# Seven dk stores as 120 rows meant to leave out DMA engine 4, with seven rows by SyncE and one in pieces, and two as 112 rows: an attention backward kernel on one core

## The chip, the cores and the metric

One core of a Trainium2 chip. The metric is the device time of one execution in microseconds (us). Faster or slower needs 2%. Each experiment was timed in three rounds beside the kernel before, and its 95% interval is given.

## The reference

The reference is the forward pass of attention with one query row per head, and its gradients:

```python
# q: (2, 32, 1, 128); k, v: (2, 32, 8192, 128); grad_out like q; all bfloat16
scores = einsum("bhqd,bhkd->bhqk", q, k) * 128 ** -0.5
p = softmax(scores); out = einsum("bhqk,bhkd->bhqd", p, v)
# returns out, dq, dk, dv
```

There are 64 heads. Each reads 2 MiB of k and 2 MiB of v and writes dk and dv of the same size. That is 8.4 MB a head and 537 MB in all.

## The kernel before

K and V of a head lie in two tiles of 128 partitions by 16 KiB. The kernel keeps twelve such tiles. The gradient overwrites the tile it is computed from and is stored from there. So the load of head i+6 has to wait until the store of head i from the same tile has landed. SyncE issues all loads, in the order of the program. GpSimd issues nearly all stores.

```python
NTILE = 12
FIRST = 6
SPREAD = range(4, 60, 7)
...
    load_eng = nc.sync
    store_eng = nc.gpsimd
...
    def by_rows(eng, dst, src, rows):
        p = 0
        for m in rows:
            pin(eng.dma_start(out=dst[p : p + m], in_=src[p : p + m], max_dma_last_dim=NT * D))
            p += m
...
    for w, a in enumerate((q, grad_out)):
        rows = a.rearrange("b h s d -> (b h s) d")
        r0 = FIRST if w == 0 else 0
        if r0:
            pin(store_eng.inc_swdge_sem([], [], mode="reset_dge_cursor"))
            pin(store_eng.dma_start(out=qd_nat[:r0, w, :], in_=rows[:r0], max_dma_last_dim=D))
        pin(load_eng.dma_start(out=qd_nat[r0:BH, w, :], in_=rows[r0:BH]))
...
    # in outer(), when the last chunk of a gradient tile is done:
            if w == 0 and i in SPREAD:
                by_rows(store_eng, dst, h.tile[w], (P - 2, 2))
            else:
                eng = load_eng if len(ends) > 1 else store_eng
                pin(eng.dma_start(out=dst[:, b0:b1, :], in_=h.tile[w][:, b0:b1, :]))
...
    # in the main loop, per head:
        if (i := at(O1 + NCH)) is not None and i + AHEAD < BH:
            load(i + AHEAD, 0)          # next k, waits for the store of dv of head i
        if (i := at(O0 + NCH)) is not None and i + AHEAD < BH:
            load(i + AHEAD, 1)          # next v, waits for the store of dk of head i
```

A plain store of 128 rows gives each of the sixteen DMA engines eight rows. The special stores of the eight heads in `SPREAD` are there for balance. The 126 rows go to fourteen engines, and the two engines that are left out get one row each. A cursor that GpSimd's transfers carry along decides which two those are. The kernel resets it at the start and moves it by a first load of six small rows.

## Time and profile before

| | before |
|---|---|
| time, median of 4 runs (lowest to highest) | 1281.13 us (1279.28 to 1284.57) |
| span of the profiled run | 1284.2 us |
| share of the DMA engines' time, loads and stores | 49.9% and 48.8% |
| DMA rate of the page | 420 GB/s |
| PE waiting for v loads | 28.8 us in 17 waits |

The lines behind the bound are shown in the prediction below. Three more are needed. The first is GB/s in forty equal slices of the span:

```profile
GB/s 388 427 428 428 428 429 428 427 428 428 428 428 428 420 428 428 428 424 426 428 428 418 425 428 428 422 418 426 428 427 419 422 429 429 426 423 429 428 413 219
```

The second is SyncE's timeline around the first special store (head 4). Its columns are start, length, engine, line and operation, and then the tile written and where it came from.

```profile
120.42 0.33 SPq L100 DMA_DIRECT2D kvt<-in_v_dram  x1
130.48 0.33 SPq L100 DMA_DIRECT2D kvt<-in_k_dram  x1
147.65 0.33 SPq L100 DMA_DIRECT2D kvt<-in_v_dram  x1
157.63 0.33 SPq L100 DMA_DIRECT2D kvt<-in_k_dram  x1
```

The third is from the view of PE's waits (us in total, number, longest).

```profile
PE tp L194 <- DMA kvt<-in_v_dram: 28.8, 17, 5.9
```

### The profile page before, as it was taken

To read this page: it belongs to the slowest core of one execution; us is meant where nothing else is said; L and a number is where in the kernel's file an instruction comes from. 1 tells how busy PE (TensorE), PEld (TensorE's weight loads), DVE (VectorE), ACT (ScalarE), POOL (GpSimd) and SP (SyncE) were. 2 spreads that over 40 slices of the span, in tenths; PEclk is the share of its full clock that TensorE was granted. 3 is DMA by queue.
4 is the path that set the end of the run, shared out by engine and by line. 5 is a ranking of instruction groups with operands and counts; after the bars stand their busy time and mean duration, and the time that the engine had idled before them with its cause. 6 is when DMAs were issued, how large, how long until landed. Compare 5 with 4: busy or idle time off the path is not lost.

```text
span 1284.2 us, 32475 instructions
## 1 busy us (share of the span) xinstructions
PE 1099.4 (86%) x14148; PEld 805.5 (63%) x14148; DVE 1014.6 (79%) x2258; ACT 956.9 (75%) x641; POOL 76.0 (6%) x143
## 2 busy tenths in 40 slices
PE   6899899899889899889899889888888799879870
PEld 5666666666666666666666666666656566656650
DVE  2888888888888888888888888888788688777882
ACT  6777777778778778778778778777778687777750
POOL 0000000000000000000000000000000000000000
PEclk9999999999999999999999999999999899999985
DMA  9999999999999999999999999999999999999995
GB/s 388 427 428 428 428 429 428 427 428 428 428 428 428 420 428 428 428 424 426 428 428 418 425 428 428 422 418 426 428 427 419 422 429 429 426 423 429 428 413 219
DMA packets 40155, 539.03 MB, mean 420 GB/s; under 512 B 5196, under 2 KB 5196, under 8 KB 6476
## 3 DMA queue, kind: packets, MB, share of 16 engines
q1 hardware_dynamic: 20172, 272.70, 49.9%
q0 software_dynamic: 19840, 264.25, 48.8%
q8 instruction: 110, 1.80, 0.5%
q14 instruction: 33, 0.27, 0.1%
HBM read 268.47 MB, written 268.47 MB: 418 GB/s over the span
## 4 chain that ended last, share of the span: by engine, by line
DVE 32%; DMA 17%; issue 14%; another core or an unknown queue 14%; PE 12%; ACT 8%; POOL 1%; SPq 0%; ACTq 0%; POOLq 0%; DVEq 0%
DVE kvt L427 18%; DMA kvt<-in_v_dram 11%; ACT ev L196 8%; PE tp L194 7%; DMA out_dram<-kvt 6%; DVE sel L395 4%; DVE rows L221 3%; DVE sel L389 1%; PE acc L372 1%; DVE pair L303 1%; PE raw L208 1%; ACT E_f L271 1%; DVE dSu L349 1%; PE sw L178 1%
## 5 line engine op out<-in xcount | busy, mean ns | idle before, releaser
L196 ACT COPY ev<-tp 128x2048 bf16<-128x2048 bf16 x512 | 941.3, 1868 | 285.7 <-PE tp L194 280.6
L427 DVE TENSOR_TENSOR kvt<-qb,pair 128x2048 bf16<-128x2048 bf16 x512 | 616.9, 1216 | 0.1
L194 PEld LDWEIGHTS <-kvt 128*128 128x128 bf16 x8192 | 507.0, 102 | 160.7 <-issue 114.4
L194 PE MATMUL tp<-ident_bf,kvt 128*128 128x128 bf16 x8192 | 572.9, 226 | 38.0 <-DMA kvt<-in_v_dram 28.8
L208 PE MATMUL raw<-ev,qdT 128*32 128x512 bf16 x2048 | 210.0, 399 | 5.0 <-ACT ev L196 1.6
L395 DVE SCALAR_TENSOR_TENSOR sel<-acc,diag,sel 128x128 f32<-128x128 f32 x384 | 134.7, 351 | 13.6
L228 PEld LDWEIGHTS sw<-sel,rows 128*128 128x128 f32 x1024 | 124.8, 192 | 29.7 <-issue 12.9
L228 PE MATMUL sw<-sel,rows 128*128 128x16 f32 x1024 | 137.2, 266 | 0.6 <-DVE rl L324 0.6
L372 PE MATMUL acc<-kvt,E_pad 128*32 128x512 bf16 x1024 | 102.9, 391 | 30.6 <-DVE E_pad L280 30.6
L445 POOL DMA_DIRECT2D out_dram<-kvt x118 | 63.3, 536 | 1081.9 <-DVE kvt L427 518.1
L372 PE MATMUL acc<-kvt,dS_pad 128*32 128x512 bf16 x1024 | 111.1, 426 | 0.8 <-DVE dS_pad L358 0.8
L221 DVE COPY rows<-raw 128x512 f32<-128x512 f32 x128 | 87.5, 684 | 26.1 <-PE raw L208 26.1
L178 PE MATMUL sw<-ident_bf,qdT 128*128 128x128 bf16 x128 | 28.5, 223 | 70.9 <-DVE mp L240 70.8
L280 DVE CAST E_pad<-E_f 128x64 bf16<-128x64 f32 x64 | 12.5, 195 | 92.9 <-ACT E_f L271 92.9
L208 PEld LDWEIGHTS <-qdT 128*32 128x32 bf16 x2048 | 64.6, 95 | 25.0 <-issue 18.4
L315 PEld LDWEIGHTS sw<-ld,ones 128*128 128x128 f32 x256 | 38.2, 188 | 54.5 <-issue 29.3
L372 PEld LDWEIGHTS <-E_pad 128*32 128x32 bf16 x1024 | 26.3, 93 | 55.2 <-DVE E_pad L280 40.1
L246 DVE TENSOR_REDUCE gm<-sw 1x1 f32<-1x128 f32 x64 | 17.9, 279 | 49.3 <-PE sw L244 49.3
L409 PE MATMUL acc<-ones,sel 128*128 128x1 f32 x256 | 47.5, 255 | 6.2 <-DVE sel L395 6.2
L315 PE MATMUL sw<-ld,ones 128*128 128x1 f32 x256 | 49.1, 261 | 0.1
L409 PEld LDWEIGHTS acc<-ones,sel 128*128 128x128 f32 x256 | 44.0, 215 | 7.3 <-DVE sel L395 7.3
L389 DVE TENSOR_SCALAR sel<-acc,diag 128x128 f32<-128x128 f32 x128 | 43.8, 342 | 0.0
(49 smaller groups left out, 367.5 us busy)
## 6 DMA issues: line engine op xcount, KB each, us to landing
out_dram<-kvt POOLq DMA_DIRECT2D x118, 2048.0 KB, 51.5
kvt<-in_v_dram SPq DMA_DIRECT2D x64, 2048.0 KB, 19.1
kvt<-in_k_dram SPq DMA_DIRECT2D x63, 2048.0 KB, 19.4
out_dram<-kvt POOLq DMA_DIRECT2D x8, 2016.0 KB, 55.7
out_dram<-kvt SPq DMA_DIRECT2D x8, 512.0 KB, 23.2
kvt<-in_k_dram SPq DMA_DIRECT2D x2, 512.0 KB, 4.5
kvt<-in_k_dram SPq DMA_DIRECT2D x1, 1024.0 KB, 7.2
out_dram<-kvt POOLq DMA_DIRECT2D x8, 32.0 KB, 55.2
```

What stands on the lines that cost most here:

```text
L194: pin(nc.tensor.transpose(tp[:, t, :], src[:, c * CH + t, :], ident_bf[:]))
L196: pin(nc.scalar.copy(out=ev[:], in_=tp[:]))
L208: nc.tensor.matmul(h.raw[g * SW : (g + 1) * SW, :], lhsT=qdT[:, w, q0 : q0 + SW], rhs=ev[:, g * QT : (g + 1) * QT, :].rearrange("p n d -> ...
L221: pin(nc.vector.tensor_copy(out=h.rows[:], in_=h.raw[:]))
L228: nc.tensor.matmul(h.score[w].rearrange("p (n t) -> p n t", t=QT)[:, :, t], lhsT=h.rows[:, t * P : (t + 1) * P], rhs=sel4[:].rearrange("p ...
L315: nc.tensor.matmul(out, lhsT=ones[:].to_broadcast([P, P]), rhs=col, start=True, stop=True)
L372: nc.tensor.matmul(h.acc[w][g : g + CW, :], lhsT=wts[:, n0 : n0 + CW], rhs=rows[:, n0 : n0 + QT, :].rearrange("p n d -> p (n d)"), start=( ...
L389: nc.vector.tensor_scalar(out=h.sel[:], in0=block, scalar1=diag[:, 0:1], scalar2=None, op0=ALU.mult)
L395: nc.vector.scalar_tensor_tensor(out=h.sel[:], in0=block, scalar=diag[:, b : b + 1], in1=h.sel[:], op0=ALU.mult, op1=ALU.add,)
L409: nc.tensor.matmul(h.acc[w][:, 0:1], lhsT=h.sel[:], rhs=ones[:], start=True, stop=True)
L427: nc.vector.tensor_tensor(out=h.tile[w][:, n0 : n0 + CH, :].rearrange("p n (e t) -> p n e t", t=2), in0=h.qb[w][:] .rearrange("p (e t) -> ...
L445: pin(eng.dma_start(out=dst[:, b0:b1, :], in_=h.tile[w][:, b0:b1, :]))
```

## The change

The change wants a finer balance. In seven heads the dk store becomes 120 rows on fifteen engines, which are to leave out engine 4. SyncE stores seven of the eight other rows on the seven lowest engines. The last row is cut: two pieces by GpSimd with 9 and 8 parts of 256 bytes (3 and 2 in head 52) are to bring the cursor back to its place, and SyncE stores the rest. In two late heads 112 rows, 2 rows and twice seven rows are to relieve two more engines.

```diff
-FIRST = 6
-SPREAD = range(4, 60, 7)
+FIRST = 5
+ONE = {4: 9, 12: 9, 20: 9, 28: 9, 36: 9, 44: 9, 52: 3}
+TWO = (57, 61)
...
-            if w == 0 and i in SPREAD:
-                by_rows(store_eng, dst, h.tile[w], (P - 2, 2))
+            if w == 0 and i in ONE:
+                by_rows(store_eng, dst, h.tile[w], (P - 8,))
+                by_rows(load_eng, dst, h.tile[w], (7,), P - 8)
+                a = 2 * ONE[i]
+                for eng, cols in (
+                    (store_eng, slice(0, a - 1, 2)),
+                    (store_eng, slice(1, a - 2, 2)),
+                    (load_eng, slice(a - 1, NT)),
+                ):
+                    pin(eng.dma_start(out=dst[P - 1 :, cols, :], in_=h.tile[w][P - 1 :, cols, :]))
+            elif w == 0 and i in TWO:
+                by_rows(store_eng, dst, h.tile[w], (P - 16, 2))
+                by_rows(load_eng, dst, h.tile[w], (7, 7), P - 14)
```

(`by_rows` gets a fifth argument, the first row. The long call in the loop is joined to one line here.)

More of the change, by code (lines that the diff above doesn't have):

```diff
@@ L83, in slot_of, with by_rows @@
         return n if n < NTILE else slot_of(i - NTILE // 2, 1 - w)
-    def by_rows(eng, dst, src, rows):
-        p = 0
+    def by_rows(eng, dst, src, rows, p=0):
         for m in rows:
@@ L440, in outer @@
             dst = (dv_v if w else dk_v)[i]
-            if w == 0 and i in SPREAD:
-                by_rows(store_eng, dst, h.tile[w], (P - 2, 2))
+            if w == 0 and i in ONE:
[7 more added lines that the diff above has]
+                ):
+                    pin(
+                        eng.dma_start(
+                            out=dst[P - 1 :, cols, :], in_=h.tile[w][P - 1 :, cols, :]
+                        )
+                    )
+            elif w == 0 and i in TWO:
+                by_rows(store_eng, dst, h.tile[w], (P - 16, 2))
+                by_rows(load_eng, dst, h.tile[w], (7, 7), P - 14)
             else:
```

## The prediction

> **What bounds the kernel now.** I read the page from the engines' table to the DMA queues, then the waits of the load queue, the DMA view in two windows, and last the busy time by stretch over the tail.
>
> ```profile
> span 1284.2 us, 32475 instructions
> PE 1099.4 (86%) x14148; PEld 805.5 (63%) x14148; DVE 1014.6 (79%) x2258; ACT 956.9 (75%) x641; POOL 76.0 (6%) x143
> ...
> DMA  9999999999999999999999999999999999999995
> ...
> q1 hardware_dynamic: 20172, 272.70, 49.9%
> q0 software_dynamic: 19840, 264.25, 48.8%
> ```
>
> No compute engine is full, while the two DMA queues (q1 the loads by SyncE, q0 the stores by GpSimd) take 98.7% of sixteen engines' span. One head moves 4 MiB in and 4 MiB out, 8.39 MB; at the 427 GB/s of the window 300 to 400 us that is 19.6 us. Undisturbed compute issues stores every 19.13 us per head (dk stores at 122.85 and 658.40 us, 28 heads apart). So DMA is slower by half a microsecond a head, and the store backlog grows. These are the store lines of the DMA view, first in the window 40 to 140 us, then 900 to 1000 us (count, KB, median us to landing):
>
> ```profile
> out_dram<-kvt POOLq DMA_DIRECT2D x9, 2048.0 KB, 17.2
> ```
>
> ```profile
> out_dram<-kvt POOLq DMA_DIRECT2D x8, 2048.0 KB, 70.5
> ```
>
> The waits of the load queue show the loop closing: a load waits until the store of the buffer that it overwrites has landed, so it waits for the slowest of the sixteen engines.
>
> ```profile
> SPq L100 <- DMA out_dram<-kvt: 1138.7, 116, 25.0
> ```
>
> A landing is sixteen completion marks, one per engine, and the trace keeps their times. For the store issued at 1176.11 us they are: five from 1193.2 to 1199.3, three from 1211.7 to 1215.7, six from 1224.0 to 1228.4, then 1232.4 and 1238.5. The engines are 45 us out of step. At 103 us the spread was only 2.4 us. The tail pays for it (columns: stretch, its length, busy time of PE, PEld, DVE, ACT, POOL, clock, DMA share, GB/s):
>
> ```profile
> 1254.00:1264.00 10.00, 2.77 (x14) 1.39 (x14) 6.82 (x13) 0.00 (x0) 0.00 (x0) 0.50 0.93 389
> 1264.00:1270.00 6.00, 0.00 (x0) 0.00 (x0) 0.00 (x0) 0.00 (x0) 0.00 (x0) 0.50 0.57 235
> 1270.00:1274.00 4.00, 0.00 (x0) 0.00 (x0) 0.00 (x0) 0.00 (x0) 0.00 (x0) 0.50 0.44 177
> 1274.00:1278.00 4.00, 0.00 (x0) 0.00 (x0) 0.00 (x0) 0.00 (x0) 0.00 (x0) 0.50 0.10 40
> 1278.00:1283.00 5.00, 0.00 (x0) 0.00 (x0) 0.00 (x0) 0.00 (x0) 0.00 (x0) 0.50 0.05 21
> ```
>
> Compute is over by 1264 us; for 19 us more a shrinking number of engines drains its backlog, the last 5 us a single one (0.05 is one of sixteen). The work left at 1264 is 6x0.57 + 4x0.44 + 4x0.10 + 5x0.05 = 5.8 us of all engines, so with that work level it would end at 1270, 13 us sooner. That is about what balance can be worth: 1%.
>
> **What the Trainium skill says.** "DMA: Bandwidth & Descriptors", section "Why a DMA increments its semaphore by 16 and not by 1": a transfer runs on the largest k up to 16 that divides its outermost dimension; SyncE's take the lowest-numbered k engines, GpSimd's with k below 16 take k consecutive ones from a cursor. The trace agrees for the special stores of before: chaining the packets end to start gives sixteen streams, and in the store at 122.85 us fourteen carry 18 packets of 8192 bytes (nine rows of 16 KiB), two carry 2. The 126 rows go to 14 engines and the 2 rows to the two left out. The cursor starts at 6 after the first query load of 6 rows, so those two are engines 4 and 5, every time.
> "Queues, rings and completion order" there says that each engine alternates between its queues by packet; the chained streams do alternate. "Latency and other measured facts" calls engines 7 and 15 usually slower; the trace here has no engine numbers, but one stream is slow: its 16 KiB packets average 624 to 630 ns against 611 to 620 of the others, and it is one of the two relieved.
>
> **The change part by part.** Unit: one row, 16 KiB. 427 GB/s over 16 is 26.7 GB/s an engine, 0.614 us a row. A plain 128-row store gives each engine 8 rows.
> Before, eight special stores: engines 4 and 5 get 1 row (-7 each time, -56), the other fourteen 9 (+8).
> After, with the cursor at 5 (first load of 5 rows), a store of 120 rows has k 15 and leaves out engine 4. The last row goes in column pieces of 256 bytes on 9 and 8 engines, which move the cursor on by 17, so that 15+17=32 brings it back to 5; that is their purpose. The rest of that row (47 columns, 12 KB) and 7 rows go by SyncE, the rows to engines 0 to 6. Seven times this: engine 4 -49; 1, 2, 3, 5, 6 +7; engine 0 +12 if the 12 KB run on it alone; 7 to 15 nothing but small pieces. The seventh moves the cursor to 9. Each of the two last stores, taken as the change's title says (14 engines, without 7 and 8, then one row each to those): 7 and 8 -7, 9 to 15 nothing, 0 to 6 +2 from SyncE's twice seven.
> Sums, before to after: engine 4 -56 to -45; 5 -56 to +11; 7 and 8 +8 to -14; 9 to 15 +8 to 0; 1, 2, 3, 6 +8 to +11; 0 +8 to +16. Times 0.614 us: 7 and 8 -13.5 us, 9 to 15 -4.9, 1, 2, 3, 6 +1.8, 0 +4.9, 4 +6.8, 5 +41.
> My reading of the groups: the eight or so early streams are 0 to 6, the late ones 7 to 15, and the last two are 7 and 8, because the change relieves just these. The first of the two last small stores ended at 1263.5 to 1267.7 us on eight engines, 1272.5 to 1274.5 on six, 1276.5 and 1282.6 on the last two. Shifted, the last comes to 1269.1, the second to 1263.0 (or 1271.6, if it is one of 9 to 15), the six to 1267.6 to 1269.6. The early streams had been idle between stores: the fastest landed 15 us after issue around 1000 us, with no backlog. They have room for what they get; engine 5 gains most and ends with the rest. So the last end moves from 1282.6 to about 1270, and I take 3 us back for what follows.
> **What it adds.** SyncE's rows stand in its order behind the next head's load, which waits for a store, and the load after that waits for these rows. A load issued with another ahead takes 19 us, so that second load starts some 10 us late, nine times. But it would have queued behind the first anyway: the loss is the gap while the load ring is empty, about 2 us, in which the engines serve stores at double pace. It costs only engines without a store backlog, or where it comes last: head 57's store delays the last v load, on the way to the end, by some 2 us. GpSimd gets three issues instead of two (0.5 us each, at 6% busy). The small pieces cost nothing to speak of.
> Sum: -12.6 + 3 = about -9.6 us on 1282.5.
>
> **The rivals.**
> 1. The 112 rows run on all 16 engines, which the skill's rule gives (16 divides 112). Then 7 and 8 get +8 to -2 (-6.1 us), 9 to 15 about the same, and the last engine ends at 1276.5: a gain of 6 us, 1277. The change's own words speak against it.
> 2. The slowest stream is not 7 or 8. It gets -4.9 us and ends at 1277.7: 1278. The trace cannot tell; that two engines trail the rest speaks for the intent.
> 3. The late loads starve compute, which from 800 us on runs just in time (waits of up to 6 us on v loads), and the end moves to the last head's compute. Nine times a full 10 us would eat everything: 1285 to 1290. Against it: 70 us of store backlog, and the ring argument above. The GpSimd queue also waited 89 us for earlier stores in nine places, and more issues may lengthen that; it too only thins the backlog.
> 4. All level, nothing lost, and the idle gaps of the early engines filled as well: 1266.
>
> **Range and chances.** The plain sum gives 1273, rivals 1 and 2 1277 to 1278, rival 4 1266, and the runs of before spread from 1279.3 to 1284.6. I predict 1273, eight in ten from 1265 to 1280. Faster by 2% needs 1257, 25.5 us, twice what the tail holds: 2%. Slower by 2% needs rival 3 thrice over: 2%. Within 2%: 96%.
>
> **What would show it.** Right: the sixteen marks of a late store within about 25 us instead of 45; the DMA share of the tail stays high and then falls at once, within some 8 us; median time to landing in the window 900 to 1000 us down from 70 to 55 or so; the mean rate up by about 3 GB/s from 420. Wrong: a single engine still draining for 5 us or more at the end (rivals 1 and 2), or long waits of PE on v loads after each special store and a lower DMA share there (rival 3).

## The result, and the profile after

The changed kernel takes 1301.36 us (median of 4 runs, 1298.96 to 1303.1), and before took 1281.13 us beside it. The ratio is 1.0153, with a 95% interval of 1.0124 to 1.0182. The predicted 1273 us and its range up to 1280 are missed by 28 and 21 us, on the other side of the kernel before. By the rule of 2% the two kernels are the same, which the prediction gave 96%; but the interval is clear of 1, so the change made the kernel slower.

First the page of the changed kernel: the span, the DMA share and GB/s in forty equal slices, and the two queues.

```profile
span 1297.2 us, 32525 instructions
...
DMA  9999999999999999999999999999999999999975
GB/s 390 426 427 430 427 427 428 426 429 427 425 429 427 425 429 422 429 429 427 428 419 428 429 427 419 413 427 428 428 420 412 429 427 426 420 409 427 428 291 207
...
q1 hardware_dynamic: 20417, 274.05, 50.0%
q0 software_dynamic: 19808, 262.90, 47.9%
```

The amount of data is the same. The rate dips to 409 to 420 in some slices, where before fell to 418 at the lowest. What is mainly new is the second-last slice, with 291 instead of 413. The stores' landing time between 900 and 1000 us (DMA view; count, KB, median us) has indeed fallen from 70.5 to about 50, which the prediction had called a sign of success:

```profile
out_dram<-kvt POOLq DMA_DIRECT2D x9, 2048.0 KB, 50.5
```

But a median hides the last engine. Below are the sixteen completion marks, in us, of one late store in the trace of the changed kernel, issued at 1051.16 us. The trace keeps one mark for each DMA engine:

```
1067.4 1067.4 1067.4 1067.6 1067.7 1067.7 1067.9 1068.1 1068.7 1068.7 1068.9 1069.0 1069.1 1069.5 | 1074.6 | 1101.0
```

Fourteen engines are level within 2.1 us, far better than in the store of before that the prediction lists. One comes 26.4 us after all others. Between the second-last and the last mark of a store, this lag is 5.2 us at 428 us, 16.0 at 743, 21.1 at 903 and 31.2 at 1164. It grows, with small dips, until then and is 24 us at 1212. The load that overwrites the tile waits for this mark.

The waits of SyncE and of PE follow. Before, SyncE's longest wait was 25.0 us and PE waited 28.8 us on v loads:

```profile
SPq L100 <- DMA out_dram<-kvt: 1109.6, 97, 42.6
```

```profile
PE tp L194 <- DMA kvt<-in_v_dram: 61.3, 28, 8.2
```

The 42.6 us has a place. SyncE's timeline at the first special store, where before had steps of 10 to 17 us:

```profile
131.05 0.33 SPq L100 DMA_DIRECT2D kvt<-in_k_dram  x1
131.47 0.33 SPq L89 DMA_DIRECT2D out_dram<-kvt  x1
131.85 0.26 SPq L451 DMA_DIRECT2D out_dram<-kvt  x1
171.44 0.37 SPq L100 DMA_DIRECT2D kvt<-in_v_dram  x1
171.91 1.11 SPq L100 DMA_DIRECT2D kvt<-in_k_dram  x1
173.19 1.38 SPq L100 DMA_DIRECT2D kvt<-in_v_dram  x1
174.67 1.44 SPq L100 DMA_DIRECT2D kvt<-in_k_dram  x1
```

SyncE issues its own seven rows (L89) and the 12 KB (L451) right behind a load. They land only at 170.0 and 171.3 us, because four loads lie ahead of them in SyncE's queue. The next load overwrites that tile, so it waits, and the loads behind it wait too. When it is free, four loads are issued within 3.2 us. I call this a hold. There are eight gaps of this kind, of 36 to 45 us.

Last the tail (stretch, length, busy time of PE, PEld, DVE, ACT, POOL, clock, DMA share, GB/s):

```profile
1264.00:1270.00 6.00, 3.87 (x40) 2.49 (x36) 4.31 (x11) 2.77 (x4) 0.55 (x1) 0.89 0.15 60
1270.00:1276.00 6.00, 3.98 (x24) 2.01 (x24) 5.67 (x13) 0.00 (x0) 0.00 (x0) 0.50 0.98 392
1276.00:1282.00 6.00, 1.88 (x11) 0.77 (x11) 5.89 (x10) 0.00 (x0) 0.00 (x0) 0.50 0.93 379
1282.00:1288.00 6.00, 0.90 (x3) 0.63 (x3) 2.57 (x8) 0.00 (x0) 0.00 (x0) 0.50 0.65 257
1288.00:1293.00 5.00, 0.00 (x0) 0.00 (x0) 0.00 (x0) 0.00 (x0) 0.00 (x0) 0.50 0.08 29
1293.00:1297.00 4.00, 0.00 (x0) 0.00 (x0) 0.00 (x0) 0.00 (x0) 0.00 (x0) 0.50 0.04 17
```

In before compute was over by 1264 us. Here the DMA engines are nearly idle from 1264 to 1270 (share 0.15) while PE still works on the last head: its v load was issued at 1240.6 us instead of 1213.5. Then the last stores run. At the very end (share 0.04, less than one of sixteen) a single engine drains.

So two things are new: one engine that falls behind, and loads that are held. Which of them makes the 20 us?

### Reading the slow engine in the trace

The trace gives no engine numbers, but packets tell. If packets are chained end to start, they fall into sixteen streams. On fifteen of them a packet of 16 KiB takes 611 ns, but for single ones that are stalled and take much longer. On one stream nearly every packet is longer, 624 to 635 ns in the mean by the stretch, and its packets of 8 KiB take some 311 to 348 ns instead of 309. Of GpSimd's packets only the rows of the special stores are cut to 8 KiB. So one can count, in every special store, how many of GpSimd's 8 KiB packets took 311 to 350 ns. Sixteen of them are the eight rows of a slow engine that was not relieved, a few are stray packets of others, and two are one row:

```
special store      1st 2nd 3rd 4th 5th 6th 7th 8th   (120, 126 or 105 rows and what GpSimd adds)
before               4   3   2   2   4   3   4   2
changed kernel       1  12  14  13  17  11  12       heads 57, 61: 14, 8
```

Before relieved the slow engine eight times out of eight, the changed kernel once out of seven. And this engine is the one that trails: seven stores have their last mark between 1040 and 1102 us in the changed kernel, and each time a store's packets on the slow stream end 0.47 to 0.49 us before it. In x5 below it is six of six between 270 and 324 us (0.45 to 0.47 us). Of SyncE's fourteen packets in each special store of the changed kernel, two were slow, in all seven (for instance 342 and 327 ns at 331 us, while the other twelve took 309), and in five of the seven stores these two started last.

### The profile page after: what moved, and what is told of

Read it like the earlier page. It is cut to its first block, busy times and chain, and to the rows that moved or that the text cites. A ratio compares the mean times of both kernels' runs of the same rounds, so it can differ in the third digit from the quotient of the medians.

```text
span 1297.2 us, 32525 instructions
## 1 busy us (share of the span) xinstructions
PE 1096.7 (85%) x14148; PEld 802.3 (62%) x14148; DVE 1016.1 (78%) x2258; ACT 958.5 (74%) x641; POOL 79.5 (6%) x151
## 4 chain that ended last, share of the span: by engine, by line
DMA 39%; DVE 25%; issue 15%; PE 10%; ACT 7%; another core or an unknown queue 2%; POOL 1%; SPq 0%; ACTq 0%; POOLq 0%; DVEq 0%
DMA out_dram<-kvt 15%; DVE kvt L427 14%; DMA kvt<-in_v_dram 14%; DMA kvt<-in_k_dram 9%; ACT ev L196 7%; PE tp L194 6%; DVE sel L395 4%; DVE rows L221 3%; PE acc L372 1%; DVE sel L389 1%; PE raw L208 1%; DVE pair L303 1%; POOL out_dram L460 1%; ACT E_f L271 1%
## 5 line engine op out<-in xcount | busy, mean ns | idle before, releaser
L372 PEld LDWEIGHTS <-E_pad 128*32 128x32 bf16 x1024 | 26.4, 93 | 52.1 <-DVE E_pad L280 36.4
```

Source lines behind the costliest of these rows:

```text
L372: nc.tensor.matmul(h.acc[w][g : g + CW, :], lhsT=wts[:, n0 : n0 + CW], rhs=rows[:, n0 : n0 + QT, :].rearrange("p n d -> p (n d)"), start=( ...
```

## The experiments

Theory at the start: the 20 us are the slow engine, which is no longer relieved, and the holds. Rivals: the holds alone; the two late special stores; SyncE as the issuer; or that a balanced run is no faster anyway.

### x5_plain: no special store at all

```diff
-SPREAD = range(4, 60, 7)
+SPREAD = ()
```

> The kernel before without any special store: all dk stores are plain 128-row stores by GpSimd, nobody is relieved and SyncE stores no rows. The lack of relief by itself. Theory (the drift, that is the missing relief of the one slow engine, is the main loss of the change; the load queue's waits behind it do harm mainly where no store backlog is left): one engine trails the others by 20 to 35 us late in the run, and the time is 1292 to 1305 us, as slow as the changed kernel or nearly. Rival (SyncE's rows are the loss): within 5 us of before.

Measured: 1294.27 us, ratio 1.0098 (1.0079 to 1.0117). As expected. No step between two loads is above 14 us, and yet one engine trails by 5.6 us at 275 us and 22 us at 1206 us. Its last stretches show the single engine:

```profile
1282.00:1287.00 5.00, 0.00 (x0) 0.00 (x0) 0.09 (x1) 0.00 (x0) 0.00 (x0) 0.50 0.09 30
1287.00:1292.00 5.00, 0.00 (x0) 0.00 (x0) 0.00 (x0) 0.00 (x0) 0.00 (x0) 0.50 0.05 18
```

Relief of the slow engine as before has it is therefore worth 12 us (before took 1281.95 us in these rounds). The size can be checked. With equal shares each engine moves 32 rows per head, 2048 in all. At 14 to 20 ns more per row (625 to 631 against 611) the slow one needs 29 to 41 us more than an engine without stalls. This is an estimate from the packet times. The 56 rows that before takes from it are 34 us of its work.

### x1_reset_sync and x2_reset_pool: relieve the slow engine every time, the last three rows by SyncE or by GpSimd

```diff
-SPREAD = range(4, 60, 7)
+SPECIAL = (4, 12, 20, 28, 36, 44, 52, 57)
-                by_rows(store_eng, dst, h.tile[w], (P - 2, 2))
+                pin(store_eng.inc_swdge_sem([], [], mode="reset_dge_cursor"))
+                by_rows(store_eng, dst, h.tile[w], (5, P - 8))
+                by_rows(load_eng, dst, h.tile[w], (3,), P - 3)      # x1
+                # x2: a second reset, then by_rows(store_eng, ..., (3,), P - 3)
```

> The kernel before with eight special dk stores (heads 4, 12, ... 52, 57) in which GpSimd's engine cursor is set back to 0 ahead of each, so that 5 rows go to engines 0 to 4 and 120 rows to the fifteen engines from 5 on, without engine 4, every time; 3 rows go by SyncE. Theory (two causes: the cursor drifted, so that the slow engine was relieved in the first special store only; and SyncE's rows queue behind the loads in SyncE's ring, so that the next load waits some 40 us): the drift is gone here and the queueing is kept. The slowest engine is no longer 20 to 37 us behind the others, but each special store still holds the load queue for 20 to 42 us, the last v load is late by some 25 us and the last head's compute ends at about 1285 us instead of 1262; time 1286 to 1295 us. Rival a (the drift alone is the loss): 1275 to 1280. Rival b (the slow stream is not engine 4): one engine still trails by over 20 us, and the time is 1295 or more.

> The same, but the 3 rows also go by GpSimd, after a second reset, so on the same engines 0 to 2. Theory: neither cause is left; no load waits longer than 25 us, the slow engine keeps up, and the time is 1274 to 1280 us, a little under before, as engines 5 to 15 carry 8 rows less per engine than before. Rival a (the drift alone): the same as the run with SyncE. Rival c (taking rows from engine 4 alone is too little, another engine bounds): at or above before's 1281.

Measured: x1 1272.17 us (ratio 0.9923, 0.989 to 0.9956), x2 1283.53 us (1.0008, 0.9968 to 1.0047). Both expectations were missed, and both the wrong way round. x1 has every hold, gaps of 35 to 40 us, and is 8 to 9 us faster than before (0.8%, under the 2%, but clear of noise). x2 has no hold and gains nothing. The page and SyncE's waits of x1:

```profile
GB/s 389 426 429 428 427 426 430 428 427 428 427 428 429 427 427 428 428 429 429 427 426 427 428 429 428 427 428 427 429 427 428 428 427 428 429 427 429 426 418 340
```

```profile
SPq L99 <- DMA out_dram<-kvt: 1121.5, 100, 39.2
```

The rate stays at 426 to 430 in all middle slices, although the queue was held for 39.2 us at the longest. No single engine trails (the last two marks are 1.3 us apart at the most), though the engines are not level: the sixteen marks of the store issued at 1033.58 us span 32 us, with ten of them in the last 6 us. This refuted the part of my theory that gave the holds a fixed price. In x2 an engine of the fast kind (packets of exactly 309 ns, with single ones of 478 to 841) trails by 10 to 21 us. Why it does so in x2 and not in x1 was not settled.

### x3_after_act: the changed kernel with SyncE's parts issued by ScalarE

```diff
-                by_rows(load_eng, dst, h.tile[w], (7,), P - 8)
+                by_rows(nc.scalar, dst, h.tile[w], (7,), P - 8)
  (likewise the 12 KB and the twice seven rows of heads 57 and 61)
```

> The changed kernel with the parts that SyncE issued given to ScalarE's own queue, which has no loads ahead of them. Theory: the load queue's waits after special stores fall from some 40 us to 10 to 15, compute ends near 1262 again, but the cursor still drifts, so the slow engine, which never idles, sets the end at about the same place: 1290 to 1300 us. Rival d (queueing alone is the loss): 1272 to 1282.

Measured: 1308.24 us, ratio 1.0204 (1.017 to 1.0239); both the theory and the rival missed. The holds are gone (steps of 14 to 17 us again, longest wait of the load queue 26.8 us), and the kernel is 7 us slower still. The trailing engine is 26.4 us behind at 1158 us. ScalarE now waits for k loads, and PE waits for ScalarE (view of the waits):

```profile
PE raw L208 <- ACT ev L196: 41.5, 13, 12.1
ACT ev L196 <- DMA kvt<-in_k_dram: 36.2, 4, 13.6
```

Taking the holds away in this manner does not mend the change. How much of the 7 us are ScalarE's waits was not taken apart.

### x4_before_strip: before with holds by one column of nine further dk stores

```diff
+            elif w == 0 and i in (5, 12, 20, 28, 36, 44, 52, 57, 61):
+                pin(store_eng.dma_start(out=dst[:, : NT - 1, :], in_=h.tile[w][:, : NT - 1, :]))
+                pin(load_eng.dma_start(out=dst[:, NT - 1 :, :], in_=h.tile[w][:, NT - 1 :, :]))
```

> The kernel before, with the last of 64 columns of nine further dk stores (heads 5, 12, ... 57, 61) issued by SyncE, on all 16 engines, cursor and balance left as they were: the queueing alone, without any drift. Theory: the nine waits of 20 to 42 us appear in the load queue, the last loads are late, compute ends some 20 us later and the time is 1290 to 1300 us. Rival a (the drift alone): within 3 us of before.

Measured: 1298.25 us, ratio 1.0123 (1.0081 to 1.0166), as expected. But these are not the holds of the changed kernel. No engine trails (the last two marks within 2 us). The gaps grow from 36 to 72 us, and the rate falls to 359 GB/s and the like:

```profile
GB/s 389 425 428 428 428 428 428 428 428 428 422 429 427 428 429 424 428 429 428 427 407 427 428 427 429 359 430 428 428 424 396 430 428 426 429 388 428 429 377 262
```

```profile
SPq L101 <- DMA out_dram<-kvt: 1138.1, 83, 69.7
```

So the rate falls in the run with holds of up to 72 us, and in x1, with 40 us, it does not. The last v load came at 1245.6 us, so the late holds at heads 57 and 61 are in the number too.

### x7_reset_sync_earlier: x1 in the heads of before (4, 11, ..., 53)

```diff
-SPECIAL = (4, 12, 20, 28, 36, 44, 52, 57)
+SPECIAL = range(4, 60, 7)
```

> The kernel with the cursor reset and 3 rows by SyncE (1272 us), its special stores moved to heads 4, 11, ... 53, as before had them, so that the last held-up load is that of head 59 and not the very last one. Theory: the hold near the end goes, the last load is issued 10 to 20 us sooner and the time is 1262 to 1271 us. Rival: the end is set by what the engines have to move, nothing changes: 1271 to 1275.

Measured: 1272.69 us, ratio 0.9933 (0.9918 to 0.9948). The last v load is issued 27 us earlier than in x1 (1189.7 instead of 1216.5 us), and the time is the same. The rival was right: with no engine trailing, the last load's time did not count. What the engines have to move fits as the limit, by estimate: 2048 rows at 0.611 us are 1251 us, and some 20 us pass at the start and the end.

### x8_no_two and x6_no_pieces: parts of the change left out

```diff
 # x8
-TWO = (57, 61)
+TWO = ()
 # x6: no pieces, the eighth row by SyncE too
-                by_rows(load_eng, dst, h.tile[w], (7,), P - 8)
-                ... the three pieces
+                by_rows(load_eng, dst, h.tile[w], (8,), P - 8)
```

> The changed kernel with heads 57 and 61 stored plainly: the seven special stores with the drift stay, the hold of the last v load goes. Theory: the last load is issued at about 1215 us instead of 1241 and compute ends 20 us sooner, but the slow engine, busy throughout, still ends last: 1293 to 1300 us. Rival (the late last load is the loss): 1275 to 1285.

> The changed kernel with the column pieces of the last row dropped: SyncE stores 8 rows instead of 7 and part of one. So nothing but the 120-row stores moves GpSimd's cursor, and it steps back by one engine per special store. Theory (the column pieces do not move the cursor, so it does so in the changed kernel too): the same time as the changed kernel, 1296 to 1305 us, and the trailing engine as far behind. If the pieces had moved the cursor as meant, this kernel would now lose the relief and be clearly slower than the changed kernel, above 1310.

Measured: x8 1297.43 us (ratio 1.0127, 1.011 to 1.0144), as expected: the two late special stores, layout and holds together, cost 4 us. In x8 the last v load is issued at 1215.2 us. x6 takes 1309.79 us (1.0227, 1.0205 to 1.0249), between the theory's upper end and the rival: partly missed. Its slow engine is unrelieved too (1 slow packet in the first special store, 7 to 15 in the others), and its gaps grow from 41 to 60 us. What the extra 8 us over the changed kernel consist of was not taken apart.

### x9, x10, x11 and x17: tiny holds

Each adds a hold and next to no data. In x9 256 bytes of each of x2's three last rows go by SyncE. In x10 sixteen pieces, one per engine, are taken from the plain kernel x5. In x11 256 bytes of each of the two last rows are taken from before. In x17 SyncE issues only three such pieces, on the three lowest engines, and GpSimd the other thirteen. x10 and x17 also store these heads as 112 and 16 rows.

```diff
 # x9, with k = 3 last rows (x11: k = 2; x10: k = 16, heads 4, 12, ..., 52, 57)
-                by_rows(store_eng, dst, h.tile[w], (3,), P - 3)
+                for eng, cols in ((store_eng, slice(0, NT - 1)), (load_eng, slice(NT - 1, NT))):
+                    by_rows(eng, dst[:, cols, :], h.tile[w][:, cols, :], (3,), P - 3)
```

> The kernel of the run with two cursor resets and no rows by SyncE (1283.5 us), except that 256 bytes of each of the three last rows go by SyncE: the same work for each engine, but the load queue is held eight times as in the run with three rows by SyncE (1272.2 us). Theory A (the hold itself moves the backlog out of the store queue into the load ring, and that is what makes the 11 us between the two runs): 1269 to 1276, load gaps of 35 to 41 us, no trailing engine. Rival B (what counts is which queue carries the three rows, or chance of the stalls): 1280 to 1287 with the same gaps, one engine trailing by 10 us or more.

> Before with every store even over the sixteen engines (1294.3 us measured without holds), and eight holds by sixteen pieces of 256 bytes, one per engine. Theory B (holds cost where one engine trails, because the held loads wait for its mark): 1297 to 1303, trailing engine's lag 20 to 25 us at 1206, load gaps 36 to 45 us. Theory A (a hold in itself is harmless or a gain): 1283 to 1294. More than 1303 would say that a hold on sixteen engines is dear by itself, as in the strip run.

> Before, with 256 bytes of each of the two last rows of its special stores by SyncE: balance of before, eight holds of the load queue. Theory A: below before, 1270 to 1278, load gaps 35 to 41 us, the marks of a store at 1176 us within 20 us instead of 45. Theory B (holds cost when there is no relief of them): 1284 to 1292. Equal to before (1278 to 1284): the holds do nothing by themselves, and the 11 us between the two reset runs come from the rows' queue.

> The plain stores with eight tiny holds (1296.8 us with one piece on each engine, 1294.3 without holds), but the pieces by SyncE on the three lowest engines, which are fast ones. If the hold costs because it waits for the slow engine: 1292 to 1295, and the gaps of the load queue fall below 40 us. If any hold costs 2 to 3 us: 1296 to 1298.

Measured, each against before of the same rounds:

| run | us | ratio (95%) | longest gaps of the loads | without the hold |
|---|---|---|---|---|
| x9 | 1272.54 | 0.9937 (0.9909 to 0.9965) | 37.6, 29.6, 24.4, then 15 to 18 | x2: 1283.53 |
| x10 | 1296.84 | 1.0118 (1.0095 to 1.014) | 42.7 to 43.0 | x5: 1294.27 |
| x11 | 1279.85 | 0.9985 (0.9959 to 1.0011) | 37.5, 30.0, 22.7, then 15 to 17 | before: 1281.96 |
| x17 | 1297.87 | 1.0125 (1.009 to 1.016) | 37.4, 26.9, then 14 to 17 | x5: 1294.27 |

Theory A was right in x9, theory B just below its range in x10, the "equal to before" case in x11, and in x17 the idea that a hold costs only by waiting for the slow engine was wrong. So a hold has no price of its own: with three balances it gained 11 us, changed nothing that the interval shows, and came with a loss of 2.6 and 3.6 us. Nor are the losses in x10 and x17 pure, for their last hold, at head 57, also delays the last v load (1241.9 and 1229.5 us; x5 1208.0).

### x12_after_reset, x13_after_cursor, x14_after_cursor_no_two: bring the cursor to 5 by small transfers

```diff
+                pin(store_eng.inc_swdge_sem([], [], mode="reset_dge_cursor"))
 # x12: five pieces of 256 bytes, strided, out of SBUF (c1 is the last column)
+                by_rows(store_eng, dst[:, c1, :], t[:, c1, :], (5,), P - 8)
 # x13, x14 instead: five rows of 128 bytes into a spare tile
+                pin(store_eng.dma_start(out=mark[:FIRST, :], in_=q_rows[:FIRST, : D // 2], max_dma_last_dim=D))
                 by_rows(store_eng, dst, h.tile[w], (P - 8,))
 # the other rows by SyncE, as seven and one; x14: TWO = ()
```

> The changed kernel with its intent about the cursor enforced: the cursor is reset ahead of each of the seven special stores, five pieces of 256 bytes bring it to 5, so that each store of 120 rows leaves out engine 4; SyncE still stores seven rows and one more, and the two last special stores are as changed. If the drift of the cursor is the failed step: 1284 to 1292 (1301.4 less the 12.6 us that one engine without relief costs), no engine trailing by over 5 us until 1160 us, load gaps still 36 to 45 us. If the holds by SyncE's rows are the main cost whatever the balance: 1297 to 1304. If the holds cost nothing once the slow engine is relieved, as in the run with three rows by SyncE: 1272 to 1280.

> The changed kernel with the cursor really at 5 in each of its seven special stores (a reset and a load of five small rows of q into a spare tile ahead of it), so that the 120 rows leave out the slow engine; SyncE stores seven rows and the eighth, the two last special stores as changed. Theory (by rows on the slow engine: 0 rows give 1294.3, plus 1 in the changed kernel 1301.4 with its holds, plus 9 in the last run 1301.2): 49 fewer rows, so no engine trails and the held loads come free with the others: 1274 to 1283, of which 3 to 4 us are the late hold of head 61. Rival (seven rows and one by SyncE cost by themselves, because SyncE's last row lies on the slow engine and holds the loads): 1290 to 1300. Sign that the cursor was moved: the trailing or slow stream carries no packets of 8 KiB of the 120-row stores by GpSimd. If it carries sixteen, the small load did not move the cursor and the run tests nothing.

> The same without the two special stores of heads 57 and 61. Theory: 3 to 4 us less than the run before it, 1271 to 1279, as in the run with three rows by SyncE (1272.2). Rival (the late hold costs nothing once the engines are level): the same as the run before it within 2 us.

Measured: x12 1301.24 us (ratio 1.0157, 1.0132 to 1.0181), x13 1302.93 (1.0165, 1.0126 to 1.0205), x14 1300.04 (1.0142, 1.0109 to 1.0174). Taken by the times alone, these runs would have cleared the cursor of blame. The trace says that they did not do what they were built for:

```
special store      1st 2nd 3rd 4th 5th 6th 7th    slow 8 KiB packets by GpSimd
x12                 12  12  12  15  16  14  16
x13                  9  10  13  15  14  16  12
x14                 13  14   8  14  15  15  16
```

The slow engine was relieved in none of the stores. Following the packets end to start in x13's first special store shows the rest: the stream that the 120 rows leave out has no slow packet and none of the five small ones, and one of the five streams with a small packet is the slow one. So the five small packets lay on five engines, and the cursor stayed at 0. That the slow engine now got one row more in each special store, instead of seven fewer, made these runs a count in the other direction (below).

### x15_after_whole, x16_after_whole_no_two: bring the cursor to 5 by five whole rows

```diff
+                pin(store_eng.inc_swdge_sem([], [], mode="reset_dge_cursor"))
+                by_rows(store_eng, dst, h.tile[w], (5, P - 8))
 # the last three rows by SyncE, the first of them as seven slices; x16: TWO = ()
```

> The changed kernel, its seven special stores as a cursor reset, five whole rows and 120 rows by GpSimd (the 120 leave out the slow engine), and three rows by SyncE, one of them cut into seven slices so that SyncE still writes 2.3 KB on each of the seven lowest engines, the slow one too; the two last special stores as changed. Theory (the relief that did not come is what failed, and holds are harmless to level engines): no trailing engine, 1274 to 1280, of which 3 us are the late hold of head 61. Rival (a hold that touches the slow engine costs by itself): 1288 to 1300. Check of the means: the slow stream carries two packets of 8 KiB in each special store, not sixteen.

> The same without the two special stores of heads 57 and 61. Theory: 2 to 4 us less than the run before it, 1271 to 1277. Rival: 1286 to 1298.

Measured: x15 1282.9 us (ratio 1.0014, 0.9975 to 1.0053), x16 1278.14 us (0.9974, 0.993 to 1.0018). The slow packets per special store are 2, 4, 3, 1, 5, 3, 2 in x15 and 4, 3, 5, 6, 4, 3, 0 in x16: the relief is real. x15 is 18 us below the changed kernel and 3 us above the theory's range. The seven slices were merged into one packet of 16,128 bytes on one engine, so the question of SyncE on the slow engine was not asked here, and that engine got three rows too many each time. The gaps grew from 41 to 59 us; that these rows are the reason was not tested.

The pair x14 and x16 differs in the relief and in how SyncE's rows lie; both have seven holds and no late special stores. The tail of x14, then of x16:

```profile
1280.00:1286.00 6.00, 1.79 (x12) 0.68 (x12) 5.53 (x9) 0.00 (x0) 0.00 (x0) 0.50 1.00 401
1286.00:1292.00 6.00, 0.60 (x3) 0.32 (x2) 0.57 (x3) 0.00 (x0) 0.00 (x0) 0.50 0.21 76
1292.00:1298.00 6.00, 0.00 (x0) 0.00 (x0) 0.00 (x0) 0.00 (x0) 0.00 (x0) 0.50 0.05 19
```

```profile
1260.00:1266.00 6.00, 2.38 (x18) 0.75 (x14) 5.82 (x15) 0.00 (x0) 0.00 (x0) 0.50 0.95 386
1266.00:1272.00 6.00, 1.88 (x11) 0.77 (x11) 5.89 (x10) 0.00 (x0) 0.00 (x0) 0.50 0.99 400
1272.00:1277.00 5.00, 0.90 (x3) 0.63 (x3) 0.76 (x4) 0.00 (x0) 0.00 (x0) 0.50 0.30 113
```

In x14 six microseconds of a single engine (0.05) end the run. In x16 the engines stop with the last head.

### x18_relief_seven_rows: real relief, and seven rows by SyncE, one on the slow engine

```diff
+                pin(store_eng.inc_swdge_sem([], [], mode="reset_dge_cursor"))
+                by_rows(store_eng, dst, h.tile[w], (5, P - 23, 11))
                 by_rows(load_eng, dst, h.tile[w], (7,), P - 7)
 # TWO = ()
```

> The seven special stores as a cursor reset, 5 rows, 105 rows (seven on each engine but the slow one) and 11 rows by GpSimd and seven by SyncE; heads 57 and 61 plain. The slow engine gets 3 rows instead of 8 each time. Theory (what counts is the relief): 1276 to 1283, beside 1278.1 of the run with 120 rows and without heads 57 and 61. Rival (held loads that wait for a SyncE row on the slow engine cost by themselves): 1286 to 1297. Check of the means: two packets of 8 KiB of 311 to 348 ns among the fourteen of SyncE in each special store, and no stream trailing with sixteen.

Measured: 1280.86 us, ratio 0.9992 (0.997 to 1.0013), as the theory had it. SyncE's fourteen packets held one or two slow ones in every special store, as in the changed kernel, and the gaps are 35 to 38 us. PE's wait on v loads is back to the level of before:

```profile
PE tp L194 <- DMA kvt<-in_v_dram: 31.8, 18, 4.6
```

So seven rows by SyncE with their holds are not what cost the 20 us. The nearest kernel without relief is x8, with the same seven rows by SyncE and seven holds, and plain heads 57 and 61 too: 1297.4 us. The 16.5 us between the two are the size of the lost relief by this pair, which still differs in the small pieces and the 12 KB.

### The sum

Rows that the slow engine got beyond its even share, counted from the layouts that the packets bear out, against the time:

| kernel | rows on the slow engine | us |
|---|---|---|
| x1, eight holds | -56 | 1272.2 |
| before, no holds | -56 | 1281.1 |
| x18, seven holds | 7 x (3 - 8) = -35 | 1280.9 |
| x16, seven holds | 7 x (1 - 8) = -49 | 1278.1 |
| x15, x16 and the late special stores | -49 + 2 = -47 | 1282.9 |
| x5, no special store | 0 | 1294.3 |
| x8, seven holds | -7 + 6 = -1 | 1297.4 |
| changed kernel | -7 + 6 + 2 = +1 | 1301.4 |
| x14, seven holds | +7 | 1300.0 |
| x13, x14 and the late special stores | +9 | 1302.9 |

In the changed kernel the -7 is the first special store with SyncE's row counted against it, the +6 are SyncE's rows in the other six, and the +2 are the late stores (7 rows of 112 and two by SyncE, against 8, twice). Every kernel with relief of 35 rows or more lies at 1272 to 1284 us, and every one without at 1294 or more, with holds or without. x12 (+9, 1301.2 us) and the other runs that the table leaves out fall on the same sides. Within each group the rows do not order the times (x3 and x6, both +1, took 1308.2 and 1309.8 us). The one exception is x4, relieved like before and at 1298.3 us, with the longest holds of all (72 us). From before to the changed kernel the 20 us divide, as far as the runs can part them, into 13 for the lost relief (before to x5), 3 for the rest of the seven special stores (x5 to x8) and 4 for the two late ones (x8 to the changed kernel). These are medians from different rounds; before's own median moved between 1280.1 and 1282.0 in them, so each share is good to a microsecond or two.

## Why the prediction was wrong

**The bound, and what balance can be worth: right.** DMA bounds the kernel, and the tail of a single engine is the loss. The prediction's 1273 us is what the kernels gave in which no single engine trails: 1272.2, 1272.7 and 1272.5 us in x1, x7 and x9. That does not confirm its row sums: these kernels have another layout, and the marks in x1 are still 32 us apart.

**The step that failed: "which move the cursor on by 17, so that 15+17=32 brings it back to 5; that is their purpose."** They did not move it. In the first special store of the changed kernel the seventeen small packets lay on nine streams, eight with two and one with one. So both pieces started on the same engine, and the cursor moved only by the 15 of the 120 rows, from 5 to 4, then 3, and so on. The trace shows where they lay: in each of the first four special stores all seven streams that carry SyncE's rows (engines 0 to 6) carry two small packets, and two further streams carry two and one. By a cursor at 4 the nine would have been engines 4 to 12, only three of the seven. In the sixth and the seventh store the stream that the 120 rows leave out, at which the cursor then stands, has no small packet. So the pieces always lay on the lowest engines and did not go by the cursor at all. Only the first store left out the slow engine. x12, x13 and x14 repeat it with two other small transfers. The term of the sum was "engine 4 -49" in the seven stores. It was -1 in those seven, and engine 4 is the one on which the time hangs. The prediction took the intent that the column pieces suggest for their effect. It had no packet of such a piece to look at in the trace of before, and it named no rival in which the cursor drifts.

**The identity of the last two engines, "7 and 8, because the change relieves just these": not shown, and not needed.** That was also read from the intent. The last engine of before is not the slow one: all six stores that landed between 600 and 660 us have their last mark from a stream whose packets take 611 ns. Which engine it is the trace does not say. The trace of before did show one slow stream, among the two that its special stores relieve. With the rule of the Trainium skill, "DMA: Bandwidth & Descriptors", section "Why a DMA increments its semaphore by 16 and not by 1", that SyncE's transfers take the lowest engines, its number follows: it gets a row of SyncE's seven (engines 0 to 6), none of SyncE's three in x1 (0 to 2), and it is the one left out by 120 rows from cursor 5, so engine 4. The change does name it.

**The 112 rows: rival 1 had the layout right.** The prediction rejected it because "the change's own words speak against it". In the first of the late special stores there were fourteen slow packets of 8 KiB, seven rows, which is 112 over sixteen. The skill's rule agreed. What it did to the time by itself no run shows.

**"That second load starts some 10 us late ... the loss is the gap while the load ring is empty, about 2 us": the size was wrong, the conclusion nearly right.** The gaps are 36 to 45 us instead of 10 to 17, because four loads lay in the queue at 130 us and not one; before's own DMA view of 40 to 140 us has loads that take 42.7 to 44.9 us to land. In before this falls to 18 to 19 us in the windows from 300 us on, which is where the prediction's 19 us come from. With holds the queue stays long, as each ends with four loads issued at once: in x1 the median load takes 37.5 to 39.4 us over the whole run. But the queue also refilled at once. In x1 and x18 such holds cost nothing that shows. For the late hold the prediction had 2 us; with and without the two late special stores the runs differ by 3.9 (x8 to the changed kernel), 2.9 (x14 to x13) and 4.8 us (x16 to x15). Rival 3, starved compute, is there in part: PE waited 32 us longer on v loads.

**Of the signs it named,** "a single engine still draining for 5 us or more at the end" was the right one for wrong. The landing time down to 50 us was named as a sign for right, and came true with the time 20 us up. The other signs for right failed: the marks at 1051 us lie 34 us apart and not 25, the mean rate of the page fell from 420 to 416 GB/s, and the tail has a stretch with a DMA share of 0.15.

**What stays open.** What decides whether a transfer of GpSimd goes by the cursor. Size does not: the kernel's own first load, five or six rows of 256 bytes, did move it, and x12's five pieces of 256 bytes did not. In all these kernels the transfers that went by the cursor had every row cut in two by `max_dma_last_dim` (the first load into 2 x 128 bytes, the whole rows into 2 x 8192), and the small ones that did not were uncut. No run varies the cut alone, so this is a hint and not shown. Why a hold gains 11 us in x9 over x2 and nothing in x11 over before. What x6 lost beyond the changed kernel. Why the last engines of before trail. And how the 3 us between x5 and x8 divide between holds and the rest.

## What to carry to other kernels

When a layout is meant to steer work away from one engine, count the packets on that engine in the trace for every such transfer, before any time is compared; a run that does not do what it was built for says nothing by its time. If a cursor has to be in a place, set it from scratch each time by transfers of the same kind as those that must obey it (here a reset and five whole rows, cut in two like the 120), and not by sums over everything in between. In a loop that waits for all sixteen engines, look at the last mark and not at the median, and then ask whether the last engine is slow or has too much to do. The version that beat both kernels, by 0.8% and 2.2%, was x1 (x7 and x9 are about half a microsecond slower): reset, 5 and 120 rows by GpSimd, the last 3 rows by SyncE, at 1272 us.

## What the Trainium skill lacked or had wrong

- "DMA: Bandwidth & Descriptors", section "Why a DMA increments its semaphore by 16 and not by 1": it says that GpSimd's transfers with k below 16 take consecutive engines from a round-robin cursor. It does state an exception, that GpSimd gives some direct copies k = 16 with the partitions spread from the first engine on, but not which copies. The small pieces here behave like it: two pieces of 9 and 8 times 256 bytes lay on the same nine streams, SyncE's seven among them, wherever the cursor stood, and five pieces of 256 or 128 bytes after a reset did not move it (8 to 16 slow packets in each of 21 stores).
- No page has the reset of the cursor, which works within a kernel: 0 to 7 slow packets per special store in the kernels that reset it and then moved it by whole rows, against 8 to 17 in the changed kernel's later stores and in x12 to x14.
- The same section's rule that k is the largest divisor up to 16 held for 112 rows: seven rows on the trailing engine, so sixteen engines.
- Section "Latency and other measured facts" calls engines 7 and 15 usually slower. Here the slow one was engine 4 by the rule above: 624 to 635 ns a 16 KiB packet in the mean against 611 without stalls, and without relief (x5) the kernel takes 12 to 13 us more than before's 1281.
- Section "Queues, rings and completion order" describes one ring per queue and engine. What it costs to put a small store behind loads on SyncE is not there: 36 to 45 us until the store of seven rows had landed and the next load could go, with about four loads of 2 MiB ahead of it.
